# A fifth pair scattered in the dense phase, later transposes on VectorE, and moved roundings in a routing attention and feed-forward kernel

## The chip, the cores and the metric

The kernel runs on one core of one Trainium2 chip. The metric is the device time of one execution in microseconds (us); of several runs the median counts.

## The reference

Routing attention over 4 batches of 8 heads, 768 positions, 64 wide, and then a bilinear feed-forward block on the 3072 rows of 512 that the attention gives. Per head, each query and each key is assigned to the nearest of 16 centroids; a query sees only the keys of its own cluster.

```python
q_assign = np.argmax(np.einsum('bhsd,hcd->bhsc', q_n, c_n), axis=-1)
k_assign = np.argmax(np.einsum('bhsd,hcd->bhsc', k_n, c_n), axis=-1)
mask = q_assign[:, :, :, None] == k_assign[:, :, None, :]
scores = scale * np.matmul(q, k.transpose(0, 1, 3, 2))
scores = np.where(mask, scores, -1000000000.0)
# softmax over the keys, then attn @ v
x = attn_out.transpose(0, 2, 1, 3).reshape(B * S, H * D)
a = x @ w_a                       # 512 x 1536
b = x @ w_b
return (a * b @ w_out)            # 1536 x 512
```

The three weights are float64; the kernel loads them as pairs of 32-bit words and rounds them to float32 itself.

## The kernel before, in words

The work comes in 16 **pairs**: one batch, two neighbouring heads, so that 2 x 64 columns fill 128 partitions. Pairs 0 to 7 (batches 0 and 1) are **dense**: all scores are computed, the mask is added through one-hot matrices, and everything is summed. Pairs 8 to 15 (batches 2 and 3) are **sorted**; below they are called pairs 1 to 8, as `n` in the code. A sorted pair's rows are scattered by cluster into DRAM, read back in cluster order, and only scores within clusters are computed.

A dense pair runs through 12 tiles of 128 keys by 384 queries (L592 scores, L602 exponential, L620 running sum on VectorE, L630 weighted values, L649 denominators). Its q and k are put across ahead of it: dense pairs 0 to 3 by TensorE (L386), pairs 4 to 7 by VectorE in 32x32 blocks (`prep_by_blocks`, L505), from q and k that were loaded in 32-wide blocks (L234). For those, the one-hot matrix goes from VectorE (L521) to its place through eight small DMAs (L525), which TensorE waits for before the pair's first scores.

A sorted pair's steps are a chain (`sorted_pair`, L1224): load rows (L1238), three groups of four TensorE transposes, each followed by a ScalarE copy (`across`, L1242 to 1254), similarities (L1260), assignment on VectorE (L1280 to 1294), prefix counts on TensorE (L1307, L1309), places on VectorE (L1320 to 1403; the steps `find`, then `after`, which ends at L1373), 24 scatters by GpSimd (`put`, L1410, indirect DMA), reload in cluster order (L1440, L1444), four VectorE transposes (L1453), scores (L1482), values (L1507, L1516), a store (L1536), 12 gathers by GpSimd (L1547) and a last transpose into the feed-forward input `xT` (L1562). Before pairs' rows can be scattered, their DRAM ring is zeroed (`clear`, L1209, from a row of zeros, `zrow`, that lies in the feed-forward input of batch 1).

Four of these pairs (`EARLY` = 4) go up to the scatter while the dense phase runs. Their room for rows lies in `wo_sb` (the place of w_out, not yet needed) and in the first half of a buffer `h` for feed-forward results (`early_room`, L1166): two row rooms, used in turn. The other four start when the dense phase is over and its memory is free (`late_room`, L1179).

The feed-forward of batch 0 runs plainly (`ffn_block`, L738): pieces of eight matmuls, for each f one with w_a (copied by ScalarE) and one with w_b, whose result VectorE multiplies in (L766, the gate product). Its first 16 pieces go in between the dense phase's groups. Its down part, and all of batches 1 to 3, use a seven-product scheme (`ffn_ups`, `ffn_downs`) whose combinations VectorE makes (L812, L824, L846 for the ups, L985, L996 for the downs). All feed-forward matmuls are issued in L709.

The weights come in 36 parts of 512 KB: 0 to 23 are w_a and w_b, 24 to 35 the twelve chunks of w_out. A part is rounded by five VectorE instructions (L310, L313, L317, L320, L328) and two of ScalarE (L324, L325). Parts 0 to 7 are due at fixed groups of the dense phase (`due`), the rest when `may_round` (L1739) allows; what is left is done at once ahead of the first down piece (`with_weights`, L1698).

The order of the instructions on each engine is fixed when the program is built. A planner in Python keeps an estimate of the time (`now`) and of each engine's load (`clocks`), and an event queue; a step is written out when its gate (`was`, `may_load`) holds and its engine's estimate is not too far ahead. So constants such as `SPACE`, `STARTS` and the times of `clear` move instructions in the engines' order; on the chip each engine takes its instructions strictly in that order and waits on semaphores. SP issues nearly all DMAs, in order, on one queue.

## Time and profile before

| what | us |
|---|---|
| median of 3 runs | 1020.98 (1020.93 to 1023.3) |
| the profiled execution | 1013.33 |
| its span, first to last instruction | 1011.6 |
| TensorE busy in the span | 969.7 |
| VectorE, ScalarE, GpSimd busy | 626.3, 280.2, 299.1 |

The profile is of one execution. Times are from the start of its span. A row of a view names the line, the engine and the operation, the tile written and the tiles read; `xN` is a count. In the chain of waits and the timeline the first number is the start, the second the length, both in us. A bracket behind a timeline row, or an arrow in the list of waits, says how long the engine stood still ahead of it and what it then got. TensorE's records count twice for a float32 matmul. The dense phase ends at about 287 us, the feed-forward of batch 0's ups at 384.

### The profile page before, as it was taken

The numbers are of one execution on the slowest core, as the hardware profiler recorded it, in microseconds if no ns is written. First come the engines' busy times: TensorE is split into PE (matmuls) and PEld (weight loads), VectorE is DVE, ScalarE is ACT, GpSimd is POOL, SyncE is SP. The second block draws the span as 40 slices with busy tenths as digits, with TensorE's granted clock in tenths as the row PEclk, the third lists the DMA queues.
The fourth block names the chain that finished last, engine by engine and source line by source line (L and its number), as shares of the span: only waits on it lengthen the run. The fifth ranks groups of instructions, "written<-read, shape, count | busy, mean of one in ns | idle before, by whom it ended". The sixth has DMA issues, their size and how long they took to land.

```text
span 1011.6 us, 20445 instructions
## 1 busy us (share of the span) xinstructions
PE 969.7 (96%) x7966; PEld 508.1 (50%) x7966; DVE 626.3 (62%) x1306; ACT 280.2 (28%) x586; POOL 299.1 (30%) x301
## 2 busy tenths in 40 slices
PE   8999888979999997999999999999999999999997
PEld 5444334433444454675545466655554665444564
DVE  6699978777694688659567844754353534334442
ACT  5766535433452332011222210022122001111100
POOL 1005535244541002434444434444444230000000
PEclk9999989999999997999999999999999999999999
DMA  6987483820248586236576369264733312212300
GB/s 182 249 229 187 93 172 98 174 58 23 71 124 162 116 169 161 99 70 150 121 178 139 101 171 171 74 135 115 149 85 84 122 34 82 56 56 59 121 33 30
DMA packets 266776, 118.86 MB, mean 117 GB/s; under 512 B 197552, under 2 KB 252848, under 8 KB 266672
## 3 DMA queue, kind: packets, MB, share of 16 engines
q1 hardware_dynamic: 257040, 104.44, 43.2%
q0 software_dynamic: 9216, 12.60, 4.8%
q8 instruction: 65, 1.06, 0.5%
q10 hardware_dynamic: 416, 0.43, 0.1%
q14 instruction: 39, 0.32, 0.1%
HBM read 79.46 MB, written 37.55 MB: 116 GB/s over the span
## 4 chain that ended last, share of the span: by engine, by line
PE 85%; DVE 11%; DMA 1%; ACT 1%; issue 1%; SPq 1%; DVEq 0%; ACTq 0%
PE m L709 65%; PE s L592 5%; PE O L630 4%; PE s L1482 2%; PE s L1507 2%; DVE acc L620 2%; PE s L1516 1%; PE m L649 1%; PE m L402 1%; SPq L525 1%; PE O L1249 1%; PE s L1562 1%; DVE rest L320 1%; PE m L1249 1%; DMA raw<-up_sums 1%
## 5 line engine op out<-in xcount | busy, mean ns | idle before, releaser
L1547 POOL DMA_INDIRECT xT<-od,idx x96 | 93.6, 975 | 127.6 <-PE m L709 121.6
L709 PE MATMUL m<-xT,wb_sb 128*64 128x384 f32 x672 | 116.2, 487 | 0.0
L709 PE MATMUL m<-xT,wa_sb 128*64 128x384 f32 x672 | 116.1, 487 | 0.1
L884 DVE TENSOR_TENSOR ha<-ha,m 128x384 f32<-128x384 f32 x72 | 39.7, 551 | 95.8 <-PE m L709 73.3
L602 ACT ACTIVATE pt<-s 128x768 f32<-128x768 f32 x96 | 74.7, 808 | 76.1 <-PE s L592 43.8
L709 PE MATMUL m<-wo_sb,h 128*64 128x256 f32 x768 | 88.0, 382 | 4.7 <-DVE wo_sb L328 4.7
L1410 POOL DMA_INDIRECT qd<-whole,idx x48 | 49.0, 1021 | 131.1 <-DVE whole L1364 66.9
L881 ACT COPY h<-m 128x384 f32<-128x384 f32 x72 | 34.5, 479 | 177.9 <-PE m L709 164.4
L709 PE MATMUL m<-raw 128*64 128x384 f32 x432 | 79.6, 488 | 1.0 <-DMA raw<-up_sums 0.8
L884 DVE TENSOR_TENSOR h<-h,m 128x384 f32<-128x384 f32 x72 | 39.6, 550 | 65.0 <-PE m L709 42.4
L709 PEld LDWEIGHTS m<-xT,wa_sb 128*64 128x64 f32 x672 | 48.1, 137 | 59.1 <-issue 51.8
L709 PEld LDWEIGHTS m<-xT,wb_sb 128*64 128x64 f32 x672 | 47.8, 137 | 58.2 <-issue 51.6
L592 PE MATMUL s<-qkT 64*128 64x384 f32 x384 | 75.1, 509 | 0.0
L630 PE MATMUL O<-pt,v 128*64 128x384 f32 x384 | 73.7, 507 | 1.1 <-ACT xT L637 1.1
L709 PEld LDWEIGHTS m<-wo_sb,h 128*64 128x64 f32 x768 | 54.5, 137 | 34.2 <-DVE wo_sb L328 5.9
L709 PE MATMUL m<-xT,h 128*64 128x256 f32 x576 | 67.4, 391 | 1.4 <-DVE xT L985 1.4
L1410 POOL DMA_INDIRECT kvd<-whole,idx x48 | 48.5, 1011 | 66.9 <-PE m L709 55.2
L1410 POOL DMA_INDIRECT qd<-h,idx x24 | 27.2, 1133 | 108.8 <-DMA qk<-in_q_dram 75.4
L709 PEld LDWEIGHTS m<-xT,h 128*64 128x64 f32 x576 | 42.1, 141 | 24.3 <-DVE xT L985 2.6
L709 PE MATMUL m<-xT,size 128*64 128x384 f32 x288 | 52.8, 487 | 0.0
L709 PEld LDWEIGHTS m<-raw 128*64 128x64 f32 x432 | 30.9, 137 | 37.3 <-issue 31.0
L881 ACT COPY ha<-m 128x384 f32<-128x384 f32 x54 | 25.9, 479 | 79.4 <-PE m L709 77.8
(269 smaller groups left out, 1502.5 us busy)
## 6 DMA issues: line engine op xcount, KB each, us to landing
whole<-kvd SPq DMA_DIRECT2D x64, 160.0 KB
raw<-in_moe_w_a_dram SPq DMA_DIRECT2D x12, 512.0 KB
raw<-in_moe_w_b_dram SPq DMA_DIRECT2D x12, 512.0 KB
raw<-in_moe_w_out_dram SPq DMA_DIRECT2D x12, 512.0 KB
raw<-up_sums SPq DMA_DIRECT2D x96, 64.0 KB
kvd<-xT SPq DMA_DIRECT2D x4, 1280.0 KB
whole<-qd SPq DMA_DIRECT2D x32, 160.0 KB
od<-whole SPq DMA_DIRECT2D x32, 160.0 KB
```

Source lines behind the costliest of these rows:

```text
L592: ins = nc.tensor.matmul(out=s[:, a, 0:HB], lhsT=Ts[p][r, S + j * P:S + (j + 1) * P], rhs=Ts[p][r, hf * HB:(hf + 1) * HB], start=start, st ...
L602: Sl.activation(out=pt, in_=s[:, :, 0:HB], func=AF.Exp, scale=SCALE)
L620: Vd.tensor_tensor(out=acc, in0=probs[u - 1] if j == 1 else acc, in1=probs[u], op=ALU.add)
L630: ins = nc.tensor.matmul(out=O_of[0][a * D:(a + 1) * D, 0:HB], lhsT=vs[p][:, a, j, :], rhs=probs[u][:, a, :], start=(j == 0), stop=(j == N ...
L709: ins = nc.tensor.matmul(out=ps[half], lhsT=lhsT[:, half], rhs=rhs, **kw)
L881: S_.copy(out=box[name], in_=box["X"][:, 0:HB])
L884: V.tensor_tensor(out=box[name], in0=box[name], in1=box[bank][:, 0:HB], op=ALU.add)
L1249: nc.tensor.transpose(out=ps[:, x * P:(x + 1) * P], in_=(M["qr"], M["kk"])[w][:, j].rearrange("p a d -> p (a d)"), identity=ident)
L1410: ins = Gi.indirect_dma_start(out=dst[:, :], out_offset=bass.IndirectOffsetOnAxis(ap=M["idx"][:, w, j, a:a + 1], axis=0), in_=src, in_offs ...
L1482: nc.tensor.matmul(out=tiles[s // 2][r0:r0 + m, s % 2, c0:c0 + m], lhsT=M["skT"][r, h, 32 * x:32 * x + m], rhs=M["sqT"][r, h, 32 * x:32 * ...
L1507: nc.tensor.matmul(out=ps[:, s, 65 * i:65 * i + 65], lhsT=pt[:, P * i:P * i + P], rhs=vt[:, i, :], start=True, stop=True)
L1547: paced(Gi.indirect_dma_start(out=M["xs"][:, j, a * D:(a + 1) * D], out_offset=None, in_=od[n][:, :], in_offset=bass.IndirectOffsetOnAxis( ...
```

## The change

- `EARLY` and `RING` go from 4 to 5: pair 5 is also loaded, assigned and scattered in the dense phase, from a third row room, the second half of the buffer `h`. The feed-forward pieces of batch 0's second block that write there wait for it, and their order changes.
- The sorted pairs after that (6 to 8) load q and k in 32-wide blocks and VectorE puts them across (two transposes of 128x768 in place of twelve TensorE transposes and three ScalarE copies); q, k and v are also loaded as rows, for the scatter.
- Roundings: the first eight parts earlier, others under new conditions, and w_out's chunks in the order 5 to 11, 0 to 4. Chunks 5 to 11 wait for the step `after` of pair 5, chunks 0 to 4 for the scatter of pair 4. The memory of the dense phase is taken over after that step of pair 5, not after the last scatter.
- Zeroing: `zrow` moves to the end of `wo_sb`; the second to fifth clears move from 40, 64, 88 (and none) to 84, 104, 140 and 190 by the planner's time, the first to its start.
- The planner leaves 1.4 us between steps that use the spare PSUM bank, and lets GpSimd issue up to 1 us behind its pace.

```diff
-    SPACE, EARLY, RING = 2.0, 4, 4
+    SPACE, EARLY, RING = 2.0, 5, 5
...
     def apart():
         if beside:
+            side_at[0] = max(side_at[0], now[0] + 1.4)
             return beside[0]
...
-        if p == HP:
-            return [[lambda: across(0), lambda: across(1)], [sims_across],
-                    assign[:2], assign[2:], [one_hot, one_hot_across], []]
         return [[lambda: across(0), lambda: across(1)], [sims_across],
-                assign, [one_hot], [one_hot_across], []]
+                assign, [one_hot, one_hot_across], [], []]
...
-            while blk == 1 and f < NF // 2 and ("put", EARLY - 1) not in done:
+            while blk == 1 and ("put", EARLY - 2 if f < NF // 2 else EARLY) not in done:
...
-    zrow = extra[:, S:S + 2 * D]
+    zrow = wo_sb.rearrange("p f n -> p (f n)")[:, NF * DM - 2 * D:]
...
-        rooms([new(ROW), t[:, 0:ROW]], new(2 * S), new(HB + 512 + 2 * (NJ + 1) * 2 * NC),
+        rooms([new(ROW), t[:, 0:ROW], t[:, ROW:]], new(2 * S), new(HB + 512 + 2 * (NJ + 1) * 2 * NC),
               new(2 * NJ * D))
...
-        parity, ring = n % 2, n % RING
+        parity, ring = 2 if n == EARLY else n % 2, n % RING
...
+        def load_blocks(w):
+            kvr = M["kvr"] = R_["kvr"][parity]
+            t = M["blocks"] = R_["blocks"][parity].rearrange(
+                "p (w j d) -> p w j d", w=2, d=32)
+            for x in range(4):
+                a, d = divmod(x, 2)
+                Qr.dma_start(
+                    out=t[32 * x:32 * x + 32, w],
+                    in_=(q, k)[w][b, 2 * hp + a, :, 32 * d:32 * d + 32].rearrange(
+                        "(j t) d -> t j d", t=32))
...
+        def block_across(w):
+            M["qkT"] = R_["qkT"].rearrange("p (w t j) -> p w j t", w=2, j=NJ)
+            if w == 0:
+                busy.append("T")
+            Vl.transpose(out=R_["qkT"][:, w * S:(w + 1) * S],
+                         in_=M["blocks"][:, w].rearrange("p j d -> p (j d)"))
...
             if n <= EARLY:
-                return was("sims", n - 1, 1) and was("put", n - 2, 1)
+                return was("sims", n - 1, 1) and (n == EARLY or was("put", n - 2, 1))
...
+        if n > EARLY:
+            chain = [plan(-48, 0, lambda: load_blocks(0), may_load, "P"),
+                     plan(FREE, 0, lambda: load_blocks(1), kind="P"),
+                     plan(FREE, 0, load_queries, kind="P"),
+                     plan(FREE, 7, lambda: block_across(0), free, "V"),
+                     plan(FREE, 0.2, lambda: block_across(1), kind="V"),
+                     plan(FREE, 0, lambda: run_chain([
+                         plan(FREE, 0, lambda a=a: load_keys(a), kind="P")
+                         for a in range(2)], now[0] + 2.0))]
+        else:
...
-                    issued[0] = max(issued[0], now[0]) + SPACE
+                    issued[0] = max(issued[0], now[0] - 1.0) + SPACE
...
-            pieces = part((6, 7, 0, 1, 2, 3, 4, 5)) + later[16:] + part((8, 9, 10, 11))
+            pieces = part(range(6)) + later[16:] + part(range(6, NF))
...
-    due = {3 * i + 1: [i] for i in range(8)}
+    due = {g: [i] for i, g in enumerate((1, 3, 4, 6, 8, 11, 15, 20))}
...
         if i < 16:
-            return idle or now[0] > ROUND + 9.0 * (i - 8)
+            return idle or now[0] > 140 + 8.0 * (i - 8)
         if i < 24:
-            return idle and now[0] > 240 or ("put", EARLY) in done
-        return idle and was("put", EARLY, 4)
-
-    ROUND = 122.0
+            return idle or bool(is_late)
+        return clocks["V"] <= now[0] + 1.4 and (
+            was("after", EARLY, 4) if i < 31 else was("put", EARLY - 1, 4))
...
-        at((0.0, 16.0, 40.0, 64.0, 88.0)[n], lambda t, n=n: clear(n))
+        at((0.0, 0.0, 84.0, 104.0, 140.0, 190.0)[n], lambda t, n=n: clear(n))
...
-        if not is_late and ("put", EARLY) in done:
+        if not is_late and ("after", EARLY) in done:
             late_room()
...
-                    for f in range(c["wo_sb"].shape[1])]
+                    for f in (5, 6, 7, 8, 9, 10, 11, 0, 1, 2, 3, 4)]
```

More of the change, by code (lines that the diff above doesn't have):

```diff
@@ L181, in short_path @@
     Gi = Clocked(nc.gpsimd, "G", 1.28, *state)
-    Q_, Qr = (Clocked(nc.sync, "P", us, *state) for us in (0.45, 0.85))
+    Q_, Qr, Qc = (Clocked(nc.sync, "P", us, *state) for us in (0.45, 0.85, 2.0))
     def pool(name, bufs, space=None, stack=ctx):
@@ L191, in short_path @@
     lists = pool("lists", 9)
-    counts = pool("counts", 4)
+    counts = pool("counts", 5)
     xtp = pool("xtp", 2)
@@ L362, in keep_busy @@
             nc.tensor.transpose(out=idle[:, 0:P], in_=ident, identity=ident)
-    banks, beside = [], []
+    banks, beside, side_at = [], [], [0.0]
     def apart():
         if beside:
+            side_at[0] = max(side_at[0], now[0] + 1.4)
             return beside[0]
@@ L1134, in short_path @@
     busy = []
-    wanted, issued, side_at = {}, [0.0], [0.0]
+    wanted, issued = {}, [0.0]
     ROW = 2 * NJ * 3 * D
@@ L1141, in rooms @@
         R_["kk"] = kk[:, 0:2 * NJ * D].rearrange("p (j a d) -> p j a d", a=2, j=NJ)
+        R_["blocks"] = [t[:, 2 * NJ * D:ROW] for t in rows]
         R_["kvr"] = [t[:, 2 * NJ * D:ROW].rearrange("p (a j d) -> p a j d", a=2, j=NJ)
@@ L1212, in clear @@
         for t, w in ((kvd[n % RING], 2 * D), (qd[n % RING], D)):
-            nc.sync.dma_start(
+            Qc.dma_start(
                 out=t[0:2 * ROWS].rearrange("(p x) d -> p x d", p=P),
@@ L1588, in may_load @@
             if n <= EARLY:
-                return was("sims", n - 1, 1) and was("put", n - 2, 1)
+                return was("sims", n - 1, 1) and (n == EARLY or was("put", n - 2, 1))
             return bool(is_late) and was("after", n - 1, 1) and was("put", n - 2, 1)
-        chain = [plan(-48 if i == 0 else FREE, 0, lambda i=i: load_rows(i, 0),
-                      may_load if i == 0 else lambda: True, "P") for i in range(2)]
-        chain += [plan(FREE, 0, lambda: run_chain([
-            plan(FREE, 0, lambda i=i: load_rows(i, 1), kind="P") for i in range(2)]))]
-        chain += [plan(FREE, (10 if n > EARLY else 7) if i == 0 else 0.3, lambda i=i: across(i),
-                       lambda: "P" not in busy and was("sims", n - 1), "T")
-                  for i in range(3)]
+        free = lambda: "P" not in busy and was("sims", n - 1)
+        if n > EARLY:
[8 more added lines that the diff above has]
+        else:
+            chain = [plan(-48 if i == 0 else FREE, 0, lambda i=i: load_rows(i, 0),
+                          may_load if i == 0 else lambda: True, "P") for i in range(2)]
+            chain += [plan(FREE, 0, lambda: run_chain([
+                plan(FREE, 0, lambda i=i: load_rows(i, 1), kind="P") for i in range(2)]))]
+            chain += [plan(FREE, 7 if i == 0 else 0.3, lambda i=i: across(i), free, "T")
+                      for i in range(3)]
         chain += [plan(FREE, 0.4, similarities, lambda: was("after", n - 1), "T")]
```

11 lines of the change are left out of this document (added).

## The prediction

> **What bounds the kernel now.** The first page says which engine is full, and its 40 slices say where it is not.
>
> ```profile
> span 1011.6 us, 20445 instructions
> PE 969.7 (96%) x7966; PEld 508.1 (50%) x7966; DVE 626.3 (62%) x1306; ACT 280.2 (28%) x586; POOL 299.1 (30%) x301
> ...
> PEclk9999989999999997999999999999999999999999
> ```
>
> TensorE (PE) is busy for 96% of the span, so only two things can shorten it: fewer TensorE instructions where it never pauses, or fewer pauses where it does. Second view, the busy time by stretches of 50 us; the columns are TensorE, its weight loads, VectorE (DVE), ScalarE, GpSimd, then the granted clock and the DMA share.
>
> ```profile
> 100.00:150.00 50.00, 41.31 (x245) 17.39 (x244) 42.69 (x77) 23.41 (x47) 21.84 (x21) 0.93 0.65 131
> 150.00:200.00 50.00, 46.40 (x291) 20.75 (x289) 41.88 (x78) 24.49 (x47) 20.42 (x18) 0.93 0.58 137
> 200.00:250.00 50.00, 42.46 (x273) 18.29 (x271) 38.95 (x76) 17.91 (x36) 19.76 (x19) 0.97 0.16 49
> 250.00:300.00 50.00, 49.11 (x308) 21.27 (x306) 37.17 (x64) 26.26 (x58) 25.79 (x24) 1.00 0.30 90
> ...
> 600.00:650.00 50.00, 50.00 (x466) 32.50 (x464) 24.10 (x54) 3.05 (x7) 19.58 (x20) 1.00 0.63 139
> ```
>
> There are two regimes. Up to about 250 us (the dense attention) TensorE and VectorE share the time and wait for each other. Later TensorE has no gap at all (50.00 of 50), and VectorE is half idle. Third view, whom TensorE waited for in the whole span:
>
> ```profile
> PE s L592 <- DMA ohT<-h: 9.5, 4, 4.6
> PE s L592 <- ACT pt L602: 5.5, 7, 2.5
> PE m L709 <- DVE wo_sb L328: 4.7, 2, 2.4
> PE m L402 <- ACT wo_sb L1315: 3.2, 1, 3.2
> ```
>
> The largest are waits for one-hot rows on their way through DMA. After a long pause the clock is granted at half for a while, so a pause costs more than its row: a mean of 0.93 over 50 us is 14% of it at half speed, 3.5 us of work lost.
>
> **Part 1, the transposes of q and k.** Each sorted pair puts q and k across in three groups of four TensorE transposes (L1249). In the change, pairs 6, 7 and 8 use VectorE, and pair 5 does its groups in the dense phase. So 12 groups leave the stretch where TensorE never pauses. The chain of waits, in order of time, has their price.
>
> ```profile
> 337.30 0.59 PE O L1249 x4
> 337.89 2.73 PE m L709 x16
> ...
> 347.26 0.79 PE O L1260 x16
> ...
> 364.97 0.29 PE O L1307
> 365.26 0.57 PE O L1309 x6
> 365.84 18.24 PE m L709 x112
> ```
>
> A feed-forward piece of 16 records takes 18.24 / 7 = 2.61 us in a row and 2.73 behind a group: a group costs 0.59 + 0.12 = 0.71 us, and twelve cost **8.5 us**. Pair 5 also takes its similarities (0.79) and prefix counts (0.29 + 0.57) along, each with such a 0.12: **1.9 us** more. Nothing else is late in their place: what TensorE does next is the following piece, whose operands lie ready. In the dense phase pair 5 costs TensorE 3 x 0.59 + 0.79 + 0.86 = **+3.4 us** at most.
>
> VectorE gets two transposes of 128x768 for each of the three pairs, and the row of the same shape is
>
> ```profile
> L505 DVE STREAM_TRANSPOSE qkT<-qk 128x768 f32<-128x768 f32 x8 | 7.3, 953 | 0.0
> ```
>
> so 6 x 0.95 = 5.7 us on an engine that has 26 of 50 us free at 600 to 650. I count it as nothing; were that cover gone, it is 5.7. SP issues 14 loads in place of 8 for such a pair and moves 1920 KB in place of 1536 (two loads of q, two of k, one of v, for 192 KB a head and tensor). At the 139 GB/s of that row the additional 384 KB are under 3 us a pair, spread over more than 50 us in which DMA is at 0.63; queued behind them on SP are reloads and stored sums. Nothing if hidden, up to 9 us in all if not; I take nothing, since before's loads of the same form fed the dense pairs through a busier queue.
>
> **Part 2, the end of the first feed-forward block.** TensorE by the timeline:
>
> ```profile
> 383.88 4.53 PE L709 MATMUL m<-wo_sb,h 128*64 128x256 f32 x40
> 390.80 0.65 PE L709 MATMUL m<-wo_sb,h 128*64 128x256 f32 x4 [2.40 <-DVE wo_sb L328]
> 393.78 1.12 PE L709 MATMUL m<-wo_sb,h 128*64 128x256 f32 x4 [2.32 <-DVE wo_sb L328]
> 396.25 8.02 PE L709 MATMUL m<-xT,h 128*64 128x256 f32 x48 [1.36 <-DVE xT L985]
> 404.11 2.76 PE L709 MATMUL m<-raw,ha 128*64 128x256 f32 x24
> 406.70 1.05 PE L709 MATMUL m<-raw,h 128*64 128x256 f32 x8
> 407.58 1.90 PE L709 MATMUL m<-size,h 128*64 128x256 f32 x16
> 409.41 0.66 PE L1249 MATMUL O<-ident,whole 128*128 128x128 f32 x4
> ```
>
> From 383.88 to 409.41 it does 144 records (40+4+4+48+24+8+16) in 25.5 us. The chain of waits has the same 144 undisturbed:
>
> ```profile
> 420.25 15.69 PE m L709 x144
> ```
>
> So the place loses 25.5 - 15.7 = **9.8 us**, the half clock after the pauses included. The cause is on VectorE:
>
> ```profile
> 384.17 0.55 DVE L766 TENSOR_TENSOR h<-ha,m 128x384 f32<-128x384 f32 x1 [2.02 <-PE m L709]
> 384.64 0.42 DVE L310 TENSOR_SCALAR wo_sb<-raw 128x512 int32<-128x512 int32 x1
> ...
> 393.64 1.02 DVE L996 TENSOR_TENSOR ha<-h 128x384 f32<-128x384 f32 x2
> 394.58 1.02 DVE L996 TENSOR_TENSOR h<-h 128x384 f32<-128x384 f32 x2
> 395.52 1.88 DVE L985 TENSOR_TENSOR xT<-wo_sb 128x512 f32<-128x512 f32 x3
> ```
>
> Three roundings of w_out (384.64 to 393.64, 3.0 us each) stand between the last gate product and the first combinations, because they were held until pair 4 was scattered. In the order of the changed kernel each stands behind an earlier gate product (room 0 is wanted last, so only f = 0 to 4 wait for pair 4) and none is left. What is late next: product (0.47), last count of pair 6 (0.69), four combinations (1.9) and three of the weights (1.8), 4.9 us after TensorE's last up piece; TensorE has two products of 24 records first, 2 x 24 x 15.69 / 144 = 5.2 us. So nothing waits. I take **-9.5 us**; bounds 0 (the weights arrive late) and -9.8.
>
> **Part 3, the dense phase.** Pair 5 brings VectorE 28 instructions; before they run late, from
>
> ```profile
> 351.36 0.58 DVE L1280 STREAM_TRANSPOSE whole<-O 128x384 f32<-128x384 f32 x1
> ...
> 381.46 0.69 DVE L1373 TENSOR_REDUCE cnt_s<-whole 128x32 f32<-128x512 f32 x1
> ```
>
> between other work, 11.0 us in sum; one rounding more is also done before the last running sum (21, were 20). These 14 us fall almost wholly into the last 50 us, where VectorE had 12.8 us idle (37.17 of 50) and TensorE 0.9. For nearly all of the phase before that, up to the 51st running sum of 64, the two orders carry the same VectorE work. Roundings come earlier in the first 50 us. What moves is which instruction is first: by durations, the four one-hots that go through DMA come 2.2, 3.7, 6.1 and 2.1 us sooner. In before their cost is
>
> ```profile
> 126.22 5.04 SPq L525 DMA_DIRECT2D ohT<-h  x8
> ```
>
> eight issues in a row, then the landing, with TensorE waiting (the 9.5 us above: 6.6 at the first, 2.9 at the second). The first wait shrinks by 2.2; the second goes, with its half clock (3.4): -8.5. The wait behind L1315 (3.2) is the end of a VectorE queue that begins with pair 4's similarities; they come one step sooner: -2. Against that: the 14 us do not fit the gaps exactly, +4; and pair 1's similarities stand straight behind the copy that they need, +0.6. I take **-6**; bounds -14 (these waits gone with their half clock) and +8 (nothing gained; just half of that idle time usable).
>
> The zeroing of the DRAM rows moves: 2 MB each (1280 + 640 KB and two small writes), until now in the first 90 us and now just ahead of the first two one-hots. Its price by SP's timeline in before, and the stretch in which the last clear there drains:
>
> ```profile
> 75.58 2.05 SPq L234 DMA_DIRECT2D qk<-in_q_dram  x4
> ...
> 83.85 4.64 SPq L1213 DMA_DIRECT2D qd<-xT  x1
> ...
> 108.04 2.05 SPq L234 DMA_DIRECT2D qk<-in_q_dram  x4
> ```
>
> ```profile
> 90.00:93.00 3.00, 3.00 (x20) 1.25 (x18) 2.93 (x5) 1.26 (x3) 2.05 (x2) 1.00 1.00 255
> ```
>
> it keeps SP for some 5 us and the DMA engines full until 93, 10 us. Ahead of the first one-hot come the second block loads (from 108.04 in before, 2 us sooner by VectorE's order at best), two loads of v, the clear and a weight part. Nearly the same list took from 75.58 to 93 in before, 17.5 us, so it drains by 124 to 126, and the one-hot's rows are issued from about 124 (126.22 less 2.2). I take nothing. The Trainium skill, DMA: Bandwidth & Descriptors, section "Queues, rings and completion order", speaks against this part: each DMA engine consumes one issuer's descriptors in ring order, so rows issued behind a clear wait for all of it. No row here shows a one-hot behind a clear; by that rule the sum would hold only if the clear is drained in time, as worked out above, and else it is the third rival.
>
> **Sum.** -8.5 - 1.9 + 3.4 - 9.5 - 6 = -22.5. The profiled execution takes 1013.33 us (span 1011.6 and 1.7 around it), so 991 on its own terms. It lies 7.65 below the median of the runs, 1020.98; I keep that distance, **998 us**.
>
> **Rivals.**
> 1. VectorE becomes the bound of the dense phase's end. For it: 14 us into 12.8 us of idle time, in order, with exponentials waiting for running sums (5.5 us already). Against it: TensorE gets 3.4 us more there too. Part 3 is then +8: -8.5 in sum, 1012.
> 2. The roundings still end the block: their loads (512 KB each) queue behind reloads and block loads on SP, and the change does not do what it says there. Part 2 is 0: -13, 1008. Against it: TensorE waited for no load there in before.
> 3. Slower: the clears hold up the first two one-hots. Each wait grows by up to 10 us plus 3.4 of half clock: 26.8 and no gain, part 3 becomes +31, the sum +15, **1036**. It decides against the change from the point where the two places wait some 16 us more than I say. Against it: the draining times above.
>
> **How the numbers follow.** Forecast 0.62, centre 998 and its own range 988 to 1004; rival 1 0.17 (1004 to 1015); rival 2 0.10 (1004 to 1011); rival 3 0.08 (1017 and over); better than 988 0.03. The range 986 to 1011 takes in the forecast, rival 2 and most of rival 1. Below 0.3% (3 us, about what a measurement of this kernel can tell from no change) lie only the edges of rivals 1 and 3: faster 0.89, same 0.03, slower 0.08.
>
> **What would show it.** Part 1: no L1249 after the dense phase, TensorE still at 50 of 50 from 450 on, its later stages shorter by 10 us. Part 2: no wait for L328, and 144 records in 16 us. Part 3: the one-hot waits under 5 us in sum, the dense phase ending within 3 us of before. Wrong would be: new TensorE waits for exponentials between 240 and 295 of over 8 us, one-hots landing more than 6 us after their last issue, or a wait for the VectorE transposes of the late pairs.

## The result: 6.5 us slower, and the profile after

The changed kernel takes a median of 1027.51 us (five runs, 1025.69 to 1029.01), before 1020.98: a ratio of 1.0053, 95% interval 1.0032 to 1.0073. The forecast was 998 us, range 986 to 1011. One of the five runs was profiled (1027.86).

The head of the page and whom TensorE waited for (engine, line, releaser: us in all, times, longest). The diff shifts line numbers: the dense scores are L590 here (L592 before), the sorted scores L1512 (L1482), the copies behind TensorE's transposes L1284 (L1254), the similarities L1290 (L1260), the feed-forward L707 (L709).

```profile
span 1026.1 us, 20378 instructions
PE 975.8 (95%) x7930; PEld 513.2 (50%) x7930; DVE 630.0 (61%) x1312; ACT 275.6 (27%) x578; POOL 302.0 (29%) x301
```

```profile
PE s L1512 <- issue: 8.3, 22, 0.5
PE O L628 <- ACT xT L635: 6.1, 5, 2.2
PE m L1279 <- ACT wo_sb L1284: 5.0, 4, 2.9
PE s L590 <- ACT pt L600: 4.5, 5, 1.6
PE s L590 <- DMA ohT<-h: 3.9, 2, 3.4
```

Three things are to be seen. The one-hot waits fell from 9.5 to 3.9 and L328 is gone, both as forecast. Waits for ScalarE's copies in the dense phase took their place (L628 was 1.1, the copies 2.5). And the longest entry is one that before's list did not have: the sorted scores stand still 22 times for nothing that the profile shows ("issue").

**The dense phase.** The timeline's row of the last dense scores, in before, in a second profile of before (see below) and in the changed kernel:

```profile
282.78 1.45 PE L592 MATMUL s<-qkT 64*128 64x384 f32 x8
```

```profile
281.95 1.45 PE L592 MATMUL s<-qkT 64*128 64x384 f32 x8
```

```profile
292.18 1.45 PE L590 MATMUL s<-qkT 64*128 64x384 f32 x8
```

It ends 9.4 us later than in the profile shown of before, where 2.6 earlier was forecast.

**The end of the first block.** TensorE's timeline of the changed kernel:

```profile
391.75 5.35 PE L707 MATMUL m<-wo_sb,h 128*64 128x256 f32 x48
396.93 5.51 PE L707 MATMUL m<-xT,h 128*64 128x256 f32 x48
402.24 2.79 PE L707 MATMUL m<-raw,ha 128*64 128x256 f32 x24
404.83 1.08 PE L707 MATMUL m<-raw,h 128*64 128x256 f32 x8
405.74 1.90 PE L707 MATMUL m<-size,h 128*64 128x256 f32 x16
407.46 0.82 PE L707 MATMUL m<-wo_sb,h 128*64 128x256 f32 x6
```

The 144 records take 407.46 - 391.75 = 15.7 us and no row has a bracket; before took 25.5. Part 2 came out (9.8 us, where 9.5 was taken), and gave back what the dense phase had lost.

**The sorted scores.** One pair's 128 records in the changed kernel, and what GpSimd did beside them:

```profile
648.58 1.99 PE L1512 MATMUL s<-whole 32*128 32x128 f32 x54
650.96 0.36 PE L1512 MATMUL s<-whole 32*64 32x64 f32 x6 [0.40 <-issue]
651.69 0.35 PE L1512 MATMUL s<-whole 32*64 32x64 f32 x5 [0.37 <-issue]
652.42 0.35 PE L1512 MATMUL s<-whole 32*64 32x64 f32 x5 [0.38 <-issue]
653.14 1.03 PE L1512 MATMUL s<-whole 32*64 32x64 f32 x58 [0.37 <-issue]
```

```profile
648.94 0.96 POOL L1440 DMA_INDIRECT kvd<-whole,idx  x1 [1.63 <-PE m L707]
650.20 0.96 POOL L1440 DMA_INDIRECT qd<-whole,idx  x1 [0.30 <-issue]
651.46 0.98 POOL L1577 DMA_INDIRECT xT<-od,idx  x1 [0.30 <-issue]
```

The profile of before has the same 128 records in one row:

```profile
657.23 2.46 PE L1482 MATMUL s<-whole 32*128 32x128 f32 x128
```

The records run freely at first (40 to 55 of them), then come two to six at a time every 0.73 us while GpSimd issues indirect DMAs, and freely again once the last of these is over, here 0.7 us after its end. This holds for seven of the eight pairs (4.2 to 5.8 us each). Beside the eighth, at 358.58, GpSimd issues nothing, and it takes 2.46. And with the end of four of these long thin stretches comes one of 3.4 us at half clock: here is the window around the pair above, and its clock mean of 0.93 over 25 us (3.5 us at half).

```profile
650.00:675.00 25.00, 22.55 (x274) 14.55 (x264) 9.10 (x20) 3.06 (x9) 9.84 (x10) 0.93 0.48 100
```

### The profile page after: what moved, and what is told of

Same layout as the page of the kernel before. It is cut to its first block, busy times and chain, and to the rows that moved or that the text cites. A ratio compares the mean times of both kernels' runs of the same rounds, so it can differ in the third digit from the quotient of the medians.

```text
span 1026.1 us, 20378 instructions
## 1 busy us (share of the span) xinstructions
PE 975.8 (95%) x7930; PEld 513.2 (50%) x7930; DVE 630.0 (61%) x1312; ACT 275.6 (27%) x578; POOL 302.0 (29%) x301
## 4 chain that ended last, share of the span: by engine, by line
PE 79%; DVE 12%; issue 2%; ACT 2%; DMA 2%; SPq 1%; DVEq 0%; ACTq 0%
PE m L707 63%; PE s L590 3%; PE O L628 3%; PE s L1512 3%; DVE acc L618 2%; PE s L1537 2%; PE s L1546 1%; PE m L647 1%; DVE rest L320 1%; ACT pt L600 1%; PE s L1592 1%; PE m L403 1%; DVE acc L674 1%; SPq L234 1%; DVE acc L667 0%
## 5 line engine op out<-in xcount | busy, mean ns | idle before, releaser
L1577 POOL DMA_INDIRECT xT<-od,idx x96 | 96.4, 1004 | 148.3 <-PE m L707 90.8
L707 PE MATMUL m<-xT,wb_sb 128*64 128x384 f32 x672 | 118.2, 493 | 0.0
L707 PE MATMUL m<-xT,wa_sb 128*64 128x384 f32 x672 | 116.2, 487 | 0.0
L707 PE MATMUL m<-wo_sb,h 128*64 128x256 f32 x768 | 88.2, 384 | 0.4 <-issue 0.4
L707 PE MATMUL m<-raw 128*64 128x384 f32 x432 | 79.2, 487 | 0.9 <-DVE comb L844 0.7
L628 PE MATMUL O<-pt,v 128*64 128x384 f32 x384 | 73.9, 508 | 6.1 <-ACT xT L635 6.1
L707 PEld LDWEIGHTS m<-xT,wb_sb 128*64 128x64 f32 x672 | 48.5, 139 | 60.2 <-issue 54.7
L1440 POOL DMA_INDIRECT qd<-h,idx x36 | 37.9, 1053 | 134.8 <-PE O L628 110.2
L707 PEld LDWEIGHTS m<-xT,wa_sb 128*64 128x64 f32 x672 | 48.0, 137 | 57.9 <-issue 53.4
L590 PE MATMUL s<-qkT 64*128 64x384 f32 x384 | 73.7, 502 | 0.0
L707 PEld LDWEIGHTS m<-wo_sb,h 128*64 128x64 f32 x768 | 55.5, 138 | 28.9 <-issue 2.8
L707 PE MATMUL m<-xT,h 128*64 128x256 f32 x576 | 65.1, 379 | 0.0
L1440 POOL DMA_INDIRECT qd<-whole,idx x36 | 37.8, 1050 | 84.0 <-DMA whole<-in_q_dram 43.1
L707 PEld LDWEIGHTS m<-xT,h 128*64 128x64 f32 x576 | 43.5, 137 | 18.9 <-issue 0.6
L707 PE MATMUL m<-xT,size 128*64 128x384 f32 x288 | 52.7, 486 | 0.0
L707 PEld LDWEIGHTS m<-raw 128*64 128x64 f32 x432 | 31.2, 137 | 39.0 <-issue 36.0
L1440 POOL DMA_INDIRECT kvd<-whole,idx x36 | 37.2, 1034 | 41.6 <-PE m L707 30.3
```

The costliest lines, as they stand in the source:

```text
L590: ins = nc.tensor.matmul(out=s[:, a, 0:HB], lhsT=Ts[p][r, S + j * P:S + (j + 1) * P], rhs=Ts[p][r, hf * HB:(hf + 1) * HB], start=start, st ...
L628: ins = nc.tensor.matmul(out=O_of[0][a * D:(a + 1) * D, 0:HB], lhsT=vs[p][:, a, j, :], rhs=probs[u][:, a, :], start=(j == 0), stop=(j == N ...
L707: ins = nc.tensor.matmul(out=ps[half], lhsT=lhsT[:, half], rhs=rhs, **kw)
L1440: ins = Gi.indirect_dma_start(out=dst[:, :], out_offset=bass.IndirectOffsetOnAxis(ap=M["idx"][:, w, j, a:a + 1], axis=0), in_=src, in_offs ...
L1577: paced(Gi.indirect_dma_start(out=M["xs"][:, j, a * D:(a + 1) * D], out_offset=None, in_=od[n][:, :], in_offset=bass.IndirectOffsetOnAxis( ...
```

## The experiments

**How the parts are summed.** From 8 us behind the last dense scores on, I count each TensorE record in the timeline from its start to the start of the next, so that pauses fall to what ran ahead of them, and add up by step. The columns are us; "dense" is the start of the last dense scores' row. The differences of two columns add up to that of their spans within 0.3 us.

| kernel | span | dense | feed-forward | transposes | similarities | prefix | scores | values |
|---|---|---|---|---|---|---|---|---|
| before, profile shown | 1011.6 | 282.8 | 641.3 | 7.0 | 3.1 | 3.5 | 20.2 | 30.1 |
| b_again | 1018.7 | 282.0 | 642.1 | 7.0 | 3.1 | 3.5 | 27.3 | 30.3 |
| changed | 1026.1 | 292.2 | 635.4 | 0 | 4.5 | 2.6 | 35.6 | 32.4 |
| b_wout | 1013.6 | 282.9 | 632.8 | 7.0 | 3.2 | 3.5 | 30.6 | 30.3 |
| a_quiet | 1013.9 | 292.9 | 634.3 | 0 | 4.5 | 2.6 | 19.1 | 37.1 |
| b_calm | 1006.4 | 286.1 | 632.7 | 8.5 | 3.2 | 3.5 | 19.1 | 30.1 |
| a_calm | 1000.3 | 291.0 | 629.7 | 0 | 4.4 | 2.6 | 19.1 | 30.1 |
| best1 | 995.6 | 287.0 | 631.0 | 0 | 2.4 | 2.6 | 19.1 | 30.1 |
| best2 | 990.7 | 280.7 | 630.0 | 0 | 3.1 | 3.5 | 19.9 | 30.1 |

Medians and ratios below are against runs of before on the same chip; each has its 95% interval.

### Before once more (b_again), no edit

> The kernel before, unchanged, profiled anew. In the profile of the changed kernel the sorted scores (64 matmuls a pair) take 4.2 to 5.8 us in seven of eight pairs, with gaps that wait for nothing shown ('issue', 8.3 us in sum), always while GpSimd issues indirect DMAs; in the one profile of before they take 2.46 to 2.9 us with no gap. Theory A: TensorE's instructions arrive slowly while GpSimd issues, in most executions of either kernel, and the profiled execution of before (1013.3 us, 7.65 under its median) was one without it. It expects here gaps of that kind at L1482, 6 to 16 us in sum with what the scores are longer, and about 1021 us. Rival B: the change brings the gaps (its 32-wide loads, its pace on GpSimd). It expects no gap at L1482 and scores of 2.46 to 2.9 us here.

Measured: 1022.74 us, ratio 1.0005 (0.9994 to 1.0015), and in this profile the gaps are there. A pair's scores and GpSimd beside them:

```profile
587.15 2.01 PE L1482 MATMUL s<-whole 32*128 32x128 f32 x57
589.54 0.35 PE L1482 MATMUL s<-whole 32*64 32x64 f32 x6 [0.37 <-issue]
590.27 1.03 PE L1482 MATMUL s<-whole 32*64 32x64 f32 x65 [0.38 <-issue]
```

```profile
587.51 0.94 POOL L1547 DMA_INDIRECT xT<-od,idx  x1 [1.64 <-PE m L709]
588.76 1.00 POOL L1410 DMA_INDIRECT qd<-whole,idx  x1 [0.30 <-issue]
```

Scores 27.3 us in place of 20.2; that is the whole difference of the two spans. So rival B falls: the gaps are no work of the change, and the one profile from which I predicted was an execution almost without them. In that one GpSimd issued beside the same seven pairs, and their scores took 2.46 to 2.90 us; so the issues alone do not always bring gaps. With the change they are longer: 35.6, three issues beside six of the pairs (b_again has two beside six, three beside one), and four stretches at half clock.

### The w_out roundings alone (b_wout)

```diff
-        return idle and was("put", EARLY, 4)
+        return clocks["V"] <= now[0] + 1.4 and (
+            was("after", EARLY, 4) if i < 31 else was("put", EARLY, 4))
...
-                    for f in range(c["wo_sb"].shape[1])]
+                    for f in (5, 6, 7, 8, 9, 10, 11, 0, 1, 2, 3, 4)]
```

> The kernel before with the w_out roundings of the change alone (chunks 5 to 11 first, after pair 4's places; chunks 0 to 4 after its scatter). The prediction's part 2 expects 9.5 us less than before, about 1011.5, no wait for L328, and the 144 records from the first down piece on in 16 us. The rival (the roundings only move and their loads queue on SP) expects within 3 us of before.

Measured: 1016.37 us, ratio 0.9948 (0.9931 to 0.9964), 5.4 us less. No wait for L328 is left, and the feed-forward column falls by 9.3 (642.1 to 632.8), as part 2 said. In this profile 3.3 of it went into longer gaps in the scores (30.6 for 27.3).

### Late transposes back on TensorE (a_tensor)

```diff
-        if n > EARLY:
+        if False:
...
-            chain += [plan(FREE, 7 if i == 0 else 0.3, lambda i=i: across(i), free, "T")
+            chain += [plan(FREE, (10 if n > EARLY else 7) if i == 0 else 0.3, lambda i=i: across(i), free, "T")
```

> The changed kernel with pairs 6 to 8 put across by TensorE again (loads of whole rows, nine late groups of four transposes). Theory A expects the gaps in the sorted scores to stay (7 to 9 us of 'issue'), and 9 x 0.71 = 6 us more than the changed kernel: about 1034. Rival B (the 32-wide loads bring the gaps) expects them gone for pairs 3 to 8: 15 us less and 6 more, about 1018.

Measured: 1020.33 us, ratio 0.9993 (0.9982 to 1.0004), 7 us less than the changed kernel: neither theory's number. The gaps stay (5.5 us of "issue" at L1512), so the 32-wide loads are not their cause; but they are shorter, scores 30.6 in place of 35.6, and no stretch at half clock follows them. Where the gaps wander with each edit, nothing of a few us can be priced. What this run did show is the similarities: 2.4 us late, where the changed kernel has 4.5.

### GpSimd quiet beside the scores (a_quiet), and beside scores and values (a_calm)

Each indirect DMA is written to wait for the newest feed-forward matmul (`paced`). In a_quiet, scores wait in the planner until no DMA is tied to the newest piece, and none is tied to it after them:

```diff
     def paced(ins):
+        tied[0] = newest[0]
...
         def scores():
+            quiet[0] = newest[0]
...
-        chain += [plan(FREE, 0.8, scores, lambda: "T" not in busy, "T"),
+        chain += [plan(FREE, 0.8, scores, lambda: "T" not in busy and tied[0] != newest[0], "T"),
...
-                        kind == "G" and (rank_ > min(wanted.values())
+                        kind == "G" and (rank_ > min(wanted.values()) or quiet[0] == newest[0]
```

In a_calm the values do the same, and GpSimd holds back as soon as either is ready:

```diff
+    def calm(n):
+        hush[0] = n
+        return tied[0] != newest[0]
+
     def paced(ins):
+        tied[0] = newest[0]
...
         def scores():
+            quiet[0], hush[0] = newest[0], None
...
         def values():
             M["O"] = R_["O"].rearrange("p (s i d) -> p s i d", s=4, d=D)
             spend(3.9)
+            quiet[0], hush[0] = newest[0], None
...
-        chain += [plan(FREE, 0.8, scores, lambda: "T" not in busy, "T"),
-                  plan(FREE, 0.6, values, kind="T"),
+        chain += [plan(FREE, 0.8, scores, lambda: "T" not in busy and calm(n), "T"),
+                  plan(FREE, 0.6, values, lambda: calm(n), "T"),
...
-                        kind == "G" and (rank_ > min(wanted.values())
+                        kind == "G" and (rank_ > min(wanted.values()) or hush[0]
+                                         or quiet[0] == newest[0]
```

> The changed kernel, with GpSimd's scatters and gathers kept from being tied to the feed-forward piece next to a pair's sorted scores, so that GpSimd issues none while the scores run. Theory A expects the sorted scores at 2.5 us a pair without gaps (15 us less) and the half clock after them gone (some 6 us less): about 1007 to 1013, if GpSimd's later issues delay nobody. Rival B expects the gaps to stay, since loads and not GpSimd bring them: 1027.

Measured: 1014.45 us, ratio 0.9918 (0.9896 to 0.9941), 13 us less than the changed kernel. All eight pairs' scores are now one row of this kind:

```profile
643.39 2.46 PE L1514 MATMUL s<-whole 32*128 32x128 f32 x128
```

The loads were not touched, so theory A stands: with at most one of GpSimd's issues beside a pair's scores, there are no gaps. Some of the gaps went on to the next step with many short matmuls, the values (its list of waits):

```profile
PE s L1548 <- issue: 4.1, 5, 1.1
```

> The changed kernel with GpSimd quiet beside scores and values, nothing else. From the kernel with the three edits (997.3) the roundings take 6 us more in the dense phase and the slower similarities 2.1: 1005. Against the calm kernel of before (1014) that is the change without gaps: 9 us faster. If the gaps were the whole miss, the prediction's sum would hold between the two: 22 us, so 992.

Measured: 1003.69 us, ratio 0.9818 (0.9796 to 0.9840). Scores 19.1 and values 30.1, no gap at either, and no stretch at half clock after the dense phase but for the last microseconds: 24 us less than the changed kernel by one rule in the planner.

### The same in the kernel before (b_wout_quiet, b_calm)

b_wout_quiet is b_wout with a first form of the rule (as in a_quiet, for values too).

> The kernel before with two edits: the w_out roundings of the change, and GpSimd kept from issuing while a pair's sorted scores and values run. With the roundings alone the scores and values took 30.6 and 30.3 us; without gaps they take 19.7 and 30. Theory A expects 1016.4 less 11, about 1006. Rival B (gaps have another cause) expects 1016.

Measured: 1026.88 us, ratio 1.0039 (1.0025 to 1.0053). Scores and values fell to 19.1 and 30.1 as expected, but GpSimd's held-back DMAs added up, and the last pair's gathers came too late:

```profile
PE s L1565 <- DMA xT<-od,idx: 18.0, 8, 4.0
```

with 20.5 us at half clock behind. A failed edit, and the price of holding GpSimd back where it ends last.

> The kernel before with GpSimd quiet beside scores and values and its pace of the changed kernel; nothing else. Theory A: scores and values 27.3 and 30.3 in the second profile of before fall to 19.5 and 30.1: 8 us less, about 1014, if the last gathers still come in time. If they don't, some 10 us more than that.

Measured: 1007.78 us, ratio 0.9849 (0.9829 to 0.9869); scores 19.1. More than the 8 us fell. GpSimd may also be 1 us behind its pace here, and this is probably why pair 4 is scattered sooner (its last scatter starts at 305.2, b_again's at 311.0); the w_out roundings come earlier with it, and the wait for L328 is gone without part 2.

So the two calm kernels compare the change without the gaps: 1003.69 against 1007.78, 4.1 us faster, and not the forecast's 22. b_calm already has most of what part 2 gives (its feed-forward column is 9.4 under b_again's), so this is the rest of the change. The spans differ by 6.1: dense phase +4.9, feed-forward -3.0, transposes -8.5, similarities +1.2, prefix -0.9.

### The dense phase: roundings (a_due), clears (a_clear), pair 5 (a_four)

```diff
-    due = {g: [i] for i, g in enumerate((1, 3, 4, 6, 8, 11, 15, 20))}
+    due = {3 * i + 1: [i] for i in range(8)}
```

> The changed kernel with the first eight roundings back at their old groups (1, 4, 7 and so on). The dense phase of the changed kernel ends 9 to 10 us later than before's, where the prediction had it 2.6 earlier. Theory D1: the early roundings crowd VectorE in the first 55 us (a stretch from 27.8 to 52.9 us, before 27.8 to 49.2) and are 3 to 4 us of that; it expects about 1024. Rival D2: pair 5 alone makes the dense phase longer; it expects 1027 to 1028.

```diff
-        at((0.0, 0.0, 84.0, 104.0, 140.0, 190.0)[n], lambda t, n=n: clear(n))
+        at((0.0, 16.0, 40.0, 64.0, 88.0, 190.0)[n], lambda t, n=n: clear(n))
```

> The changed kernel with the clears of pairs 1 to 4 back at their old times, so that none stands ahead of the first two one-hots on SP. The changed kernel waits 3.9 us for one-hot rows in all (before 9.5). The theory that the clears cost nothing there expects 1026 to 1029. The prediction's third rival (clears hold up one-hots) expects the wait of 3.4 us and the half clock behind it gone, 5 us or more: 1022.

```diff
-    SPACE, EARLY, RING = 2.0, 5, 5
+    SPACE, EARLY, RING = 2.0, 4, 4
...
-        rooms([new(ROW), t[:, 0:ROW], t[:, ROW:]], new(2 * S), new(HB + 512 + 2 * (NJ + 1) * 2 * NC),
+        rooms([new(ROW), t[:, 0:ROW]], new(2 * S), new(HB + 512 + 2 * (NJ + 1) * 2 * NC),
...
-            pieces = part(range(6)) + later[16:] + part(range(6, NF))
+            pieces = part((6, 7, 0, 1, 2, 3, 4, 5)) + later[16:] + part((8, 9, 10, 11))
...
```

Four conditions that name `EARLY` go back with these lines.

> The changed kernel with pair 5 late again (four early pairs, a ring of four, two row rooms, the old order of the feed-forward pieces); pairs 5 to 8 are put across by VectorE, and roundings and clears stay as changed. Rival D2 expects the dense phase to end 8 to 9 us earlier, and the late stages to grow by pair 5's similarities and prefix (2.4, its operands in the slower layout): 6 us less, about 1021. Theory D1 expects 3 to 4 us less in the dense phase at most, so 1026.

Measured: a_due 1024.45 us (ratio 1.0018, 1.0006 to 1.0030), a_clear 1027.95 (1.0064, 1.0045 to 1.0084), a_four 1026.88 (1.0043, 1.0028 to 1.0058). The medians carry the gaps (scores 36 to 37 in all three), so the last dense scores' rows are read. In a_due and a_four:

```profile
286.29 1.45 PE L590 MATMUL s<-qkT 64*128 64x384 f32 x8
```

```profile
281.81 1.45 PE L590 MATMUL s<-qkT 64*128 64x384 f32 x8
```

Against the changed kernel's 292.18, the old roundings give back 5.9 us and a late pair 5 gives back 10.4, in one execution each. Other runs show how far such a number carries. Through the dense phase a_calm, a_quiet, a_tensor and a_clear have the changed kernel's order of instructions on TensorE, VectorE and ScalarE, and start their last dense scores at 290.0 to 292.9; a_pace (below), with the same order, starts them at 296.2. With the old roundings it is 286.3 to 288.3 (a_due, best1, best1_tensor), with both edits 280.7 (best2). So the roundings are about 4 us and a late pair 5 is 6 to 10.

Where the time goes is seen from the starts of the 9th, 33rd, 77th and 95th of the 96 dense score tiles, which lie at 28, 89, 231 and 283 us in before. The three columns are the stretches between them, in us:

| kernel | 28 to 89 | 89 to 231 | 231 to 283 |
|---|---|---|---|
| before, profile shown | 61.2 | 141.8 | 51.6 |
| b_again | 60.8 | 141.2 | 51.8 |
| changed | 66.5 | 140.1 | 57.5 |
| a_calm | 65.1 | 140.2 | 57.6 |
| a_clear | 64.2 | 140.0 | 58.2 |
| a_due | 61.3 | 139.0 | 58.0 |
| a_four | 64.1 | 137.8 | 50.9 |

The early roundings (D1) cost their time in the first stretch, in every kernel of the table that has them. Pair 5 (D2) costs its 6 us in the last one: its own TensorE records stand there, and TensorE waits 3.5 us in place of 0.9, never for an exponential. The stretch between them, where the one-hots were waited for in before, hardly became shorter.

**The clears.** In the changed kernel the first one-hot stands behind a clear and a weight part on SP:

```profile
125.73 4.39 SPq L299 DMA_DIRECT2D raw<-in_moe_w_b_dram  x1
126.92 0.58 DVE L522 STREAM_TRANSPOSE h<-h 128x384 bf16<-128x384 bf16 x1
130.23 5.20 SPq L526 DMA_DIRECT2D ohT<-h  x8
135.77 0.50 PE L590 MATMUL s<-ohT 64*128 64x384 bf16 x1 [3.40 <-DMA ohT<-h]
```

VectorE has it ready at 127.50, and SP issues it 2.7 us later. In a_clear SP issues it at once, and TensorE waits 0.6 us for it in place of 3.4:

```profile
126.28 0.58 DVE L522 STREAM_TRANSPOSE h<-h 128x384 bf16<-128x384 bf16 x1
126.92 5.04 SPq L526 DMA_DIRECT2D ohT<-h  x8
132.56 0.50 PE L590 MATMUL s<-ohT 64*128 64x384 bf16 x3 [0.58 <-DMA ohT<-h]
153.07 0.66 PE L1279 MATMUL m<-ident,h 128*128 128x128 f32 x4 [3.57 <-ACT acc L652]
```

So the clear does hold up the first one-hot. But the time is not gained: a_clear is 6.6 us ahead of the changed kernel at 147 us, then waits 3.6 us for ScalarE (the last row), with 3.4 us at half clock behind, and is 1.7 ahead at 165 and at the phase's end. Its median is the changed kernel's. One wait taken away came back as another.

How a rounding can cost TensorE 2 us where VectorE has the same work in all is to be read in the changed kernel's timeline, first at 35 us:

```profile
35.06 0.43 DVE L310 TENSOR_SCALAR wa_sb<-raw 128x512 int32<-128x512 int32 x1 [2.69 <-DMA raw<-in_moe_w_a_dram]
35.06 0.69 ACT L324 ACTIVATE size<-raw 128x512 f32<-128x512 f32 x1 [0.52 <-DMA raw<-in_moe_w_a_dram]
37.18 1.51 ACT L600 ACTIVATE pt<-s 128x768 f32<-128x768 f32 x2
38.05 0.34 PE L590 MATMUL s<-ohT 64*128 64x384 bf16 x2 [1.65 <-ACT pt L600]
```

VectorE and ScalarE both stand at the rounding until its weights arrive; the exponentials stand behind it on ScalarE, TensorE behind these, and half clock follows. And at 58 us:

```profile
58.30 0.42 DVE L310 TENSOR_SCALAR wa_sb<-raw 128x512 int32<-128x512 int32 x1
63.27 0.58 DVE L674 STREAM_TRANSPOSE acc<-inv 128x384 f32<-128x384 f32 x1
63.88 0.21 ACT L688 ACTIVATE inv<-inv 128x12 f32<-128x12 f32 x1 [4.60 <-DVE acc L674]
64.09 0.46 ACT L635 COPY xT<-O 128x384 f32<-128x384 f32 x1
64.61 1.51 PE L628 MATMUL O<-pt,v 128*64 128x384 f32 x8 [2.21 <-ACT xT L635]
```

A rounding of 3 us ahead of the denominators' chain (L667 to L680) makes ScalarE wait in L688, and the copy that frees TensorE's next bank (L635) stands behind it.

### GpSimd's pace (a_pace), and the quiet kernel with TensorE's transposes (a_quiet_tensor)

```diff
-                    issued[0] = max(issued[0], now[0] - 1.0) + SPACE
+                    issued[0] = max(issued[0], now[0]) + SPACE
```

> The changed kernel without its last small edit: GpSimd may not issue up to 1 us behind its pace. In the changed kernel three indirect DMAs run beside most pairs' sorted scores, where two run in before, and four of the eight are followed by 3.4 us at half clock. Theory P: the pace edit packs GpSimd's issues together, and this is what makes the gaps longer than in before. It expects two issues beside the scores, scores of some 28 us in place of 35.6, at most one stretch of half clock there: 8 to 14 us less, 1014 to 1020. Rival: the issues beside the scores are set by where the vector transposes put the chain, not by the pace; it expects 1025 to 1029.

Measured: 1026.54 us, ratio 1.0031 (1.0021 to 1.0042), scores 35.4. The time is the rival's; the mechanism is not settled. In the profile (1030.16 us, the slowest of the ten) pairs 2 to 8 have one or two issues beside their scores, as Theory P said, and take 2.5 to 5.2 us. But pair 1, which had none, has five, takes 8.7 us from 357.46 on, and has 17 us at half clock from 361 on. So the pace moves the issues, and here their harm fell elsewhere. Which edits put a third issue beside the scores was not separated.

> The changed kernel with GpSimd quiet beside the scores and with pairs 6 to 8 put across by TensorE again. With the gaps out of the way this prices the prediction's part 1 for three pairs: 9 groups x 0.71 = 6.4 us. Less the similarities that read vector-transposed q and k in 1.58 us in place of 0.79 (3 x 0.79 = 2.4), 4 us more than the quiet changed kernel is expected: 1018.5. The rival, that the 32-wide loads cost something of their own (DMA, SP), expects no more than 1014.5.

Measured: 1023.43 us, ratio 1.0007 (0.9996 to 1.0019), 9 us over a_quiet, not 4. Its values take 40.0 (a_quiet 37.1), with four stretches at half clock (a_quiet one): a price that the gaps hide again. Inconclusive, and the reason for the kernels without any gap.

### Three edits together (best1, best2), and part 1 without gaps (best1_tensor)

best1 is the changed kernel with the rule of a_calm, the roundings of a_due, and this order of the 32-wide loads, after which the similarities' operands lie side by side:

```diff
-                    out=t[32 * x:32 * x + 32, w],
+                    out=t[32 * x:32 * x + 32, w].rearrange("p (j c) d -> p j c d", c=4),
                     in_=(q, k)[w][b, 2 * hp + a, :, 32 * d:32 * d + 32].rearrange(
-                        "(j t) d -> t j d", t=32))
+                        "(c t j) d -> t j c d", c=4, t=32))
...
-            M["qkT"] = R_["qkT"].rearrange("p (w t j) -> p w j t", w=2, j=NJ)
+            M["qkT"] = R_["qkT"].rearrange("p (w j t) -> p w j t", w=2, j=NJ)
```

best2 is best1 with the edits of a_four, best1_tensor best1 with those of a_tensor in place of the new load order.

> The changed kernel with GpSimd quiet beside scores and values both, the first eight roundings at their old groups, and the 32-wide loads in the order that lets the similarities read q and k without a stride (the same 128-byte pieces). From the quiet changed kernel's 1014.5: 6 us of the dense phase, 2.4 of the similarities (0.79 each again) and 4 to 7 of the values: about 1001. If the similarities stay at 1.58, the stride was not their cause.

> As the kernel beside it, with pair 5 late again (four early pairs). Rival D2 (pair 5 costs VectorE more in the dense phase than it saves later) expects less than that kernel: 4 us earlier at the end of the dense phase, 3 us more late, 1000. Against it: GpSimd's issues then end some 40 us later, and if the last gathers come after TensorE's need for them, it is slower by the wait (18 us and its half clock in the kernel of before with quiet scores): 1020.

> The kernel with the three edits, but with pairs 6 to 8 put across by TensorE. With no gaps in either, the prediction's price (0.71 us a group) makes it 9 x 0.71 = 6.4 us slower: 1003.7. If the vector transposes or the 32-wide loads have a cost of their own, it is less.

Measured: best1 997.28 us, ratio 0.9747 (0.9730 to 0.9764); best2 992.90, ratio 0.9706 (0.9686 to 0.9725); best1_tensor 1001.81, ratio 0.9790 (0.9769 to 0.9811). best1 and best2 came out lower than expected (1001 and 1000); best2 is 3% under before. The groups of the late similarities, in the changed kernel and in best1 (busy, mean ns of one):

```profile
L1290 PE MATMUL O<-whole,cTb 128*32 128x192 f32 x48 | 4.7, 523 | 0.0
```

```profile
L1295 PE MATMUL O<-whole,cTb 128*32 128x192 f32 x48 | 2.6, 332 | 0.0
```

The stride was the cause. Pairs 6 to 8 on VectorE are worth 4.5 us between best1_tensor and best1 (4.4 by the ratios, as the two ran on different chips), where the prediction's price gave 6.4; the transposes themselves are 5.3 in best1_tensor's timeline. What takes the last microsecond back is open. And best2's head shows the whole run fed and nearly always at full clock:

```profile
span 990.7 us, 20376 instructions
PE 957.3 (97%) x7918; PEld 500.3 (51%) x7918; DVE 633.5 (64%) x1314; ACT 272.7 (28%) x574; POOL 297.2 (30%) x301
PEclk9999989999999999999999999999999999999999
```

Its gathers came in time, so GpSimd's later end did no harm; D2 holds here too (dense phase 6.3 us shorter, late stages 1.5 longer).

## Why the prediction was wrong, point by point

- **Part 1** (-8.5 for twelve groups, -1.9 for pair 5's similarities and prefix): the direction was right. The transposes column falls by 7.0, so a group is 0.59; the 0.12 behind each would lie in the feed-forward column, where it cannot be told apart. Pair 5's 0.8 and 0.9 went. Missed: the similarities of pairs 6 to 8 read q and k with a step of six elements, 24 bytes, and take twice as long (4.5 us for the three, not 2.4: +2.1). The diff showed that step; I priced the transposes and not the reader of their result. The Trainium skill has the rule, in SBUF — State Buffer, section "Door 1: The DMA port swizzle": consecutive accesses to the same 16-byte line run at full bandwidth, and for float32 it gives 4 as the stride that is free. The two rows above agree as far as they go (steps of six and one; none between was run).
- **Part 2** (-9.5): right, -9.3 by itself and -9.8 in the changed kernel.
- **Part 3** (-6, bounds -14 to +8): this step failed. The phase became 9.4 longer; with +3.4 for pair 5's TensorE work, part 3 was +6.0. Two of its terms were wrong. First, the waits for one-hots and behind L1315 were priced as time gained, -10.5. The one-hot waits did fall as forecast (9.5 to 3.9), but the stretch in which they all stood became only 1.8 shorter: others took their place, as a_clear shows for one of them. Second, "Roundings come earlier in the first 50 us" stood there without a price, beside the sentence that the two orders "carry the same VectorE work" up to the 51st running sum. That says nothing of what stands ahead of what: roundings moved to where their weights had not landed, or ahead of a chain that frees a bank. The first stretch became 5.3 longer than in the profile shown of before, of which the runs give the roundings some 4. Pair 5's own price held: 3.4 for TensorE and 4 for work that does not fit were taken, and the last stretch became 5.9 longer.
- **Rival 1** (VectorE becomes the bound of the phase's end, part 3 at +8) is near in number only. By the prediction's own sign it would have shown over 8 us of new waits for exponentials between 240 and 295; there are none.
- **Rival 2** (the roundings still end the block) was rightly held to be unlikely. **Rival 3** (the clears hold up the one-hots) came in part, against the draining time of "124 to 126" that was worked out: the DMA engines were at 0.95 or more of their time from 124 to 132, still at 0.85 to 134, and the first one-hot was issued 2.7 us late. The second was not held up. The price was wrong the other way: a_clear takes that wait away and gains nothing that its median shows. Whether the rows also waited in a ring behind the clear cannot be told apart here from SP's late issue.
- **The gaps** were in no term. "Later TensorE has no gap at all" was read from one execution, and the 7.65 us between it and the median of its own kernel was carried along as an offset, without asking what it was. It was this: the second profile has 7.0 us more in the scores. In the changed kernel the scores and values grew by another 10.4 (57.6 to 68.0), and the half clock behind them is most of the 5.7 by which its feed-forward is longer than a_calm's.

Together, against the second profile of before: the forecast was -22.5, the spans differ by +7.4. Of these 29.9 us the dense phase has 12.8 (10.2 for -2.6), scores and values 10.4, the feed-forward 2.8 (-6.7 for -9.5, the half clock included), similarities and prefix 2.4 (+0.5 for -1.9) and the transposes 1.5 (-7.0 for -8.5). What stays open: by which mechanism GpSimd's issues thin out TensorE's instructions. The runs show that the gaps come only beside these issues and go with them. They do not show where inside the chip they arise, whether the issuing does it or the transfers that it starts, nor why one execution of before had hardly any.

## What to carry to other kernels

When a profiled execution lies well under the median of its own kernel, find what the others have and it lacks before building a sum on it. Moving work within an in-order engine is not free because the total stays: for each moved instruction ask what it waits for and what stands behind it, on that engine and on the next. A wait that goes is worth its length only if nothing else is as late: look for the next one before pricing it. And where a layout changes, price every later reader of it.

## What the runs showed of the hardware

- Sorted scores are 128 short records in 2.46 us. While GpSimd issues indirect DMAs (0.96 us each, 0.30 apart), TensorE gets past 40 to 55 of them and then only two to six every 0.73 us, with no semaphore to wait for. So it is wherever two or more issues run beside the scores, but not in the first profile of before; DMA was at 0.48 in the window shown. Long matmuls (0.16 us a record) do not show it: 32 feed-forward records of 128x384 take 5.16 us in the median of 24 stretches of the changed kernel with GpSimd issuing for over half of the time, and the same in 28 stretches with no issue beside them.
- Four of the seven long stretches in the changed kernel ended in 3.4 us at half clock, though no single gap in them is over 0.5 us.
- A float32 matmul whose moving operand has a step of 24 bytes takes 523 ns in the mean where the same with adjacent elements takes 332, twice per group of sixteen (1.58 and 0.79 us).
- With the DMA engines full, SP's own issue is slow: in the changed kernel the weight part behind a clear takes 4.39 us to issue at 125.73 (0.33 at 60.69), and the one-hot behind it on SP goes out 2.7 us after it is ready.
